# Expert 0 runs to its end before expert 1 begins, its first wait is shortened, and TensorE gets filler products in two short waits

## The chip, the core and the metric

The program runs on one core of one Trainium2 chip. A core has a matrix engine (TensorE, PE in the rows), a vector engine (VectorE, DVE), a scalar engine (ScalarE, ACT), a general engine (GpSimd, POOL) and a queue engine (SyncE, SP), each with its own instruction stream, and 16 DMA engines. The metric is the device time in microseconds (us), lower is better: 508.98 us before, the median of three runs (508.8 to 509.01).

## The reference

Three stages follow one another. All are computed in float32 by the reference.

```python
# 1. attention, (2 batches, 8 heads, 768 rows, 64 wide); rows attend to rows of the same 6-bit bucket
mask   = q_bucket[..., :, None] == k_bucket[..., None, :]
scores = np.where(mask, scale * q @ k.T, -1e9)
x      = softmax(scores) @ v                        # -> x: (1536 tokens, 512)
# 2. experts: each token goes to one of 8
e_idx  = np.argmax(x @ w_gate, axis=1)
for e in range(8):
    h = np.maximum(x[e_idx == e] @ w1[e], 0.0)      # 512 -> 1024
    out[e_idx == e] = gate_w * eom[:, e] * (h @ w2[e])   # 1024 -> 512
# 3. a dense layer on all tokens
h    = out @ w_in;  s = h * softmax(h)              # 512 -> 1024
y    = ((s - mean) / sqrt(var + 1e-6) * g_ln) @ w_out     # 1024 -> 512
```

The weights w_in and w_out arrive as 64-bit floats and are decoded on the chip from their two 32-bit halves.

## The kernel before

Every product is taken as three 16-bit products (high x high, high x low, low x high), so each operand exists as a pair hi/lo. All five engines run from an instruction order that the code writes out by hand (`manual_schedule`); each engine works through its own list in that order and stops at the head of it when an operand isn't there.

**From attention to the experts.** After the last attention unit the last three token tiles (9, 10, 11) are routed one after the other: the logits (`fin_l`), the arg-max as a one-hot mask (`route_a`), counts by products with triangular and all-ones matrices (`route_mm`), then the row of each token in a scratch table `xs` (`route_b`), into which GpSimd scatters the tokens. Expert 0's tokens are not read back from that table: TensorE collects them itself. `gather_first` adds what was read early, and `gather_mm` (written `gm`) multiplies the tiles 6 to 11 by masks `gx["oh"]` which VectorE and ScalarE build (`oh`, lines 970 to 973). On this way TensorE waits twice for a mask, ahead of `gm(6, ...)` and ahead of `route_mm(3, ...)`. The four sums lie in four PSUM banks; `gather_copy` copies them out to `xw`, sums 0 and 3 on ScalarE (line 1000), sums 1 and 2 on VectorE (line 998). Sums 0 and 3 lie in the two halves of one two-bank tile.

**The experts.** The list `seq` names the order of products: `m1` is an expert's first layer (`mm1`, lines 1255 to 1257), `m2` its second (`mm2`, lines 1284 to 1286). Each is cut into four groups `g`, and each (kind, expert, group) is a slot of the loop, 64 slots in all. A first layer's group sums over the four 128-wide parts `kk` of the 512 inputs, three products each, for two blocks of 128 outputs; its result lies in one PSUM bank of a pool of eight (`ps_x`, used in turn). `ev1` makes the hidden values: ScalarE writes hi (line 1263), and one slot later VectorE writes lo (line 1264, collected in `late`). `ev2` does the same for the second layer and writes into `yT` at a column that stands in a register; these eight registers (`starts`, line 1307) are loaded on VectorE and ScalarE from the counts in `slot_i`.

**What streams beside them.** In slot `i` the loop converts a quarter `prep[i]` of a weight matrix (ScalarE hi, line 168; VectorE lo, line 172), and issues on SP the load of the quarter that is due three slots later (`w_load`, five buffers `raw`). `WD` gives the slots at which the 13 remaining pieces of w_in and w_out are decoded: ScalarE line 126, GpSimd line 131, VectorE lines 136, 142 and 147, then hi on GpSimd and lo on VectorE; their loads go out six slots ahead. `x_load(n)` (line 1164) fetches expert n's tokens from `xs` by a transposing DMA on SP. GpSimd also scatters the gate of each token tile during the first three second layers (line 1382).

## Time and profile before

| | us |
|---|---|
| median of three runs | 508.98 |
| the profiled execution's own time | 509.42 |
| its span, first to last instruction | 507.6 |
| TensorE busy in it | 493.2 (97%) |
| VectorE, ScalarE, GpSimd busy | 385.1, 319.1, 283.2 |
| attention and routing, to TensorE's first product of an expert | 0 to 242.01 |
| experts | 242.01 to 376.40 |
| dense layer, to TensorE's last product | 376.40 to about 501 |

The times of the stages are where TensorE begins their products. A matmul row's length is a modelled latency; many are in flight at once, so the spacing of the starts is what one costs. Idle times and what ended them stand in square brackets at the end of a row.

### The profile page before, as it was taken

How to read it: one execution, taken by the hardware profiler on the slowest of the kernel's cores; microseconds unless marked ns; L12 is line 12 of the kernel's file. 1: busy time of each engine (PE TensorE's matmuls, PEld its weight loads, DVE VectorE, ACT ScalarE, POOL GpSimd, SP SyncE). 2: the span in 40 equal slices, each digit the busy share in tenths (PEclk: the TensorE clock that was granted, in tenths of full speed). 3: DMA queues.
4: the chain of work that ended last, by engine and by line, in shares of the span. 5: the costliest groups of instructions: out<-in, count | busy, mean ns of one | idle time of the engine just before them, and what ended most of it. 6: DMA issues, size and time to landing. Idle time of an engine off the chain costs nothing. (4 is left out here: it accounts for less than half of the span.)

```text
span 507.6 us, 12505 instructions
## 1 busy us (share of the span) xinstructions
PE 493.2 (97%) x4716; PEld 378.0 (74%) x4716; DVE 385.1 (76%) x914; ACT 319.1 (63%) x602; POOL 283.2 (56%) x447
## 2 busy tenths in 40 slices
PE   7899999999999999999999999999999999999994
PEld 5678787878777777787999999999974444444443
DVE  7788788878989788777698889799965986656610
ACT  6878887888778787885256574578714365444421
POOL 7989899969779898825356457320242113221131
PEclk9999999999999999999999999999999999999998
DMA  8665375988765764501599999999710236432281
GB/s 265 111 207 114 122 151 149 273 171 254 133 243 109 229 156 126 152 1 64 154 263 339 253 286 270 246 311 342 267 46 0 57 69 126 101 87 62 62 146 41
DMA packets 107182, 83.21 MB, mean 164 GB/s; under 512 B 80624, under 2 KB 89456, under 8 KB 107120
## 3 DMA queue, kind: packets, MB, share of 16 engines
q1 hardware_dynamic: 104736, 76.09, 58.5%
q0 software_dynamic: 2304, 6.31, 3.3%
q8 instruction: 37, 0.61, 0.5%
q14 instruction: 25, 0.20, 0.1%
q10 hardware_dynamic: 80, 0.00, 0.0%
HBM read 51.43 MB, written 9.97 MB: 121 GB/s over the span
## 5 line engine op out<-in xcount | busy, mean ns | idle before, releaser
L654 ACT ACTIVATE p<-s,mx 128x768 f32<-128x768 f32 x96 | 95.7, 997 | 24.3 <-DVE mx L643 12.1
L639 DVE TENSOR_REDUCE mx<-s 128x1 f32<-128x768 f32 x96 | 90.8, 946 | 22.3 <-PE s L628 19.6
L668 ACT COPY pt<-t 128x384 f32<-128x384 f32 x192 | 82.0, 480 | 17.7 <-PE t L666 16.2
L666 PE MATMUL t<-ident,p 128*128 128x128 f32 x576 | 78.8, 273 | 0.5 <-ACT pt L668 0.2
L666 PEld LDWEIGHTS t<-ident,p 128*128 128x128 f32 x576 | 68.7, 141 | 10.0 <-ACT pt L668 1.0
L690 PE MATMUL v<-pt,v 128*64 128x128 f32 x1128 | 71.9, 277 | 0.0
L131 POOL TENSOR_SCALAR dm<-dm 128x512 f32<-128x512 f32 x16 | 34.2, 2138 | 60.0 <-ACT dm L126 60.0
L690 PEld LDWEIGHTS v<-pt,v 128*64 128x64 f32 x1128 | 60.6, 137 | 7.8 <-issue 6.0
L1484 PE MATMUL o<-wo,zT 128*128 128x512 f16 (+1 forms) x312 | 63.7, 363 | 0.1
L1284 PE MATMUL a<-hh,wb 128*128 128x224 f16 (+5 forms) x256 | 63.4, 251 | 0.1
L1412 PE MATMUL h<-wi,yT 128*128 128x512 f16 x288 | 63.5, 379 | 0.0
L1285 PE MATMUL a<-hh,wb 128*128 128x224 f16 (+5 forms) x256 | 63.4, 251 | 0.0
L1286 PE MATMUL a<-hh,wb 128*128 128x224 f16 (+5 forms) x256 | 63.4, 251 | 0.0
L1256 PE MATMUL a<-xw,wa 128*128 128x224 f16 (+5 forms) x224 | 55.1, 249 | 0.0
L1255 PE MATMUL a<-xw,wa 128*128 128x224 f16 (+5 forms) x224 | 55.1, 249 | 0.0
L1257 PE MATMUL a<-xw,wa 128*128 128x224 f16 (+5 forms) x224 | 55.1, 249 | 0.0
L1484 PEld LDWEIGHTS <-zT 128*128 128x128 f16 x312 | 30.5, 98 | 32.2 <-issue 0.4
L1412 PEld LDWEIGHTS <-yT 128*128 128x128 f16 x288 | 28.2, 98 | 33.7
L628 PE MATMUL s<-k,q 128*128 128x384 f16 x192 | 47.4, 328 | 1.7 <-ACT p L654 1.5
L628 PE MATMUL s<-b,cm 128*128 128x384 f16 x192 | 47.0, 326 | 1.1 <-DVE b L590 1.1
L1490 POOL DMA_INDIRECT out_dram<-o,tok x12 | 12.6, 1046 | 53.3 <-issue 42.4
L168 ACT ACTIVATE wa<-raw 128x1024 f16<-128x1024 f32 x24 | 25.3, 1055 | 19.2 <-DMA raw<-in_moe_w_dram 19.1
(278 smaller groups left out, 1011.3 us busy)
## 6 DMA issues: line engine op xcount, KB each, us to landing
raw<-in_moe_w_dram SPq DMA_DIRECT2D x64, 512.0 KB, 5.4
raww<-in_moe_w_in_dram SPq DMA_DIRECT2D x8, 512.0 KB, 6.5
raww<-in_moe_w_out_dram SPq DMA_DIRECT2D x8, 512.0 KB, 8.2
xs<-raw SPq DMA_DIRECT2D x8, 448.0 KB, 6.8
v<-in_v_dram SPq DMA_DIRECT2D x8, 384.0 KB
q<-in_q_dram SPq DMA_DIRECT2D x6, 384.0 KB, 4.8
k<-in_k_dram SPq DMA_DIRECT2D x6, 384.0 KB
cm<-q SPq DMA_DIRECT2D x14, 96.0 KB, 2.1
```

The lines of the kernel that those rows point to most:

```text
L628: nc.tensor.matmul(t[:, c, 0:SB], d[x, h][:, s], flat(d[y, h])[:, c * SB:(c + 1) * SB], start=first, stop=not first)
L639: nc.vector.tensor_reduce(out=mx[:, 0:1], in_=t[:, :, 0:SB], op=ALU.max, axis=AX.XY)
L654: nc.scalar.activation(out=p, in_=s_t.pop(i)[:, :, 0:SB], func=AF.Exp, scale=mx[:, 1:2], bias=mx[:, 2:3], accum_out=sums[j][:, qt, h:h + 1])
L666: nc.tensor.transpose(t[:, g * 128:(g + 1) * 128], p[:, c, g * 128:(g + 1) * 128], ident)
L668: nc.scalar.copy(out=pt[i][:, 3 * c:3 * c + 3], in_=t[:, 0:SB].rearrange("p (g c) -> p g c", g=3))
L690: nc.tensor.matmul(o[64 * h:64 * h + 64], vt[:, h, c], ph[h][:, c], start=(c == 0), stop=(c == NS - 1), tile_position=(0, 64 * h))
L1255: nc.tensor.matmul(ps[:, i, 0:n], w[:, 0, kk, fs], xw[:, 0, kk], start=(kk == 0), stop=False)
L1284: nc.tensor.matmul(ps, w[:, 0, f, ds], hh[:, 0, f], start=(f == 0), stop=False)
L1285: nc.tensor.matmul(ps, w[:, 0, f, ds], hh[:, 1, f], start=False, stop=False)
L1286: nc.tensor.matmul(ps, w[:, 1, f, ds], hh[:, 0, f], start=False, stop=(f == KF - 1))
L1412: nc.tensor.matmul(ps[:, c], yT[:, a, kk, ts], w_i[:, w, kk, c * 512:(c + 1) * 512], start=(kk == 0 and a == 0 and w == 0), stop=(kk == KD ...
L1484: nc.tensor.matmul(ps, zT[:, KF * a + f], w_o[:, w, f, cs], start=(f == 0 and a == 0 and w == 0), stop=(f == KF - 1 and a == 1))
```

## The change

Five things are edited.

- `emit_pv` keeps the second bank of its last PSUM tile as `gx["spare"]`, and a new function `keep_on(n)` multiplies the 16-bit identity by itself n times into it. It is called with 10 ahead of `gm(6, ...)` and with 6 ahead of `route_mm(3, ...)`. Nothing reads these products.
- Ahead of the first `mm1` two tiles of the eight-bank pool are taken and one element of each is set to zero on VectorE, so that expert 0's first group falls on the third bank. For expert 0 the parts `kk` are summed in the order 0, 1, 3, 2.
- `seq` runs expert 0's second layer directly behind its first; expert 1's first layer follows. The weight quarters of w2 for expert 2 now come ahead of those of w1 for expert 3, and `x_load(4)` moves to the third group of expert 2's first layer.
- The column registers are loaded one by one, each at the start of its expert's second layer, and not all eight ahead of the loop.
- Nine of the 13 decoding slots in `WD` move by 2 to 5 slots.

```diff
@@ emit_pv
-                pv[j, 2] = ps_s.tile([128, 2, 512], F32, tag="s", name="s")[:, 0]
+                t = ps_s.tile([128, 2, 512], F32, tag="s", name="s")
+                pv[j, 2], gx["spare"] = t[:, 0], t[:, 1, 0:128]
@@ new
+        def keep_on(n):
+            for _ in range(n):
+                nc.tensor.matmul(gx["spare"], ident16, ident16, start=True, stop=True)
@@ the order ahead of the experts
             a_("route_s")(2)
+            a_("keep_on")(10)
             gm(6, range(4))
             a_("route_a")(3)
             oh(8, True)
+            a_("keep_on")(6)
             a_("route_mm")(3, tail=True)
@@ mm1
+        for _ in range(2):
+            spare = ps_a.tile([128, 2, CAP], F32, tag="a", name="a")
+            nc.vector.memset(spare[0:1, 0, 0:1], 0.0)
...
+            ks = (0, 1, 3, 2) if e == 0 else range(KD)
...
-                for kk in range(KD):
+                for kk in ks:
@@ the experts' loop
-        starts = [nc.values_load(slot_i[0:1, 2, e:e + 1], engines=[ET.DVE, ET.Activation], min_val=0, max_val=NT,
-                                 skip_runtime_bounds_check_because=why) for e in range(E)]
-        seq = [("m1", 0), ("m1", 1)]
-        for e in range(E - 2):
+        starts = {}
+        def start(e):
+            starts[e] = nc.values_load(slot_i[0:1, 2, e:e + 1], engines=[ET.DVE, ET.Activation], min_val=0, max_val=NT,
+                                       skip_runtime_bounds_check_because=why)
+        seq = [("m1", 0), ("m2", 0), ("m1", 1), ("m1", 2)]
+        for e in range(1, E - 2):
...
-        order = [("w1", 2), ("w1", 3), ("w2", 2)]
+        order = [("w1", 2), ("w2", 2), ("w1", 3)]
...
-        WD = [0, 2, 6, 10, 14, 18, 22, 27, 32, 54, 58, 62, 66]
+        WD = [4, 7, 10, 14, 18, 22, 26, 30, 34, 54, 58, 62, 66]
...
-            n = 3 if (kd, e, g) == ("m1", 0, 2) else e + 4 if (kd, g) == ("m2", 3) else E
+            n = {("m1", 0, 2): 3, ("m1", 2, 2): 4}.get((kd, e, g), e + 4 if e and (kd, g) == ("m2", 3) else E)
...
             else:
+                if g == 0:
+                    start(e)
                 mm2(e, g, CAPS[e])
```

Three places show what this does to the order. First TensorE where the experts begin, before the change: the last product of the count (line 896) and the first products of expert 0. `raw` holds the collected tokens, `wa` the weights; the engine named in brackets is one whose work the instruction waits for.

```order
L896 MATMUL m<-hs,ones_74 128x8 [waits PE_49]
L1255 LDWEIGHTS wa [waits PE_49]
L1255 MATMUL a<-raw,wa 128x224 [waits Activation_49]
...
L1255 MATMUL a<-raw,wa 128x224 [waits DVE_49]
...
L1255 MATMUL a<-raw,wa 128x224 [waits DVE_49]
```

And the same place in the changed kernel, where the product's line is 1268:

```order
L897 MATMUL m<-hs,ones_74 128x8 [waits DVE_49]
L1268 LDWEIGHTS wa
L1268 MATMUL a<-raw,wa 128x224 [waits Activation_49]
...
L1268 MATMUL a<-raw,wa 128x224 [waits DVE_49]
...
L1268 MATMUL a<-raw,wa 128x224 [waits Activation_49]
...
L1268 MATMUL a<-raw,wa 128x224 [waits DVE_49]
```

Before, one wait for ScalarE stands at the first product and covers both of its copies; now the first product waits for one copy and the third part has a wait for ScalarE of its own.

Second, ScalarE between the last gate (`reo`) and expert 0's hidden values (`hh`), before the change:

```order
L882 ACTIVATE reo<-rosel 128x1
L1307 TENSOR_LOAD slot_i x8
L126 ACTIVATE dm<-raww 128x512
L1263 ACTIVATE hh<-a 128x448 x2
L126 ACTIVATE dm<-raww 128x512
L1263 ACTIVATE hh<-a 128x448 x2
L168 ACTIVATE wa<-raw 128x1024
```

and in the changed kernel:

```order
L883 ACTIVATE reo<-rosel 128x1
L1276 ACTIVATE hh<-a 128x448 x4
L168 ACTIVATE wa<-raw 128x1024
L126 ACTIVATE dm<-raww 128x512
L1323 TENSOR_LOAD slot_i
L168 ACTIVATE wa<-raw 128x1024
```

The eight register loads and two decoding steps no longer stand ahead of or between expert 0's four hidden groups, and one register load stands behind them.

Third, SP's queue late in the experts, around the fetch of expert 6's tokens, before the change (line 184 loads quarters of w2 of expert 4, line 182 of w1 of expert 6, line 116 a piece of w_out):

```order
L184 DMA raw<-in_moe_w_dram 128x2x512
L116 DMA raww<-in_moe_w_out_dram 128x1024
L184 ISA
L184 DMA raw<-in_moe_w_dram 128x2x512
L1164 ISA
L1164 DMA_TRANSPOSE xw<-xs 128x8x224
L184 ISA
L184 DMA raw<-in_moe_w_dram 128x2x512
L182 ISA
L182 DMA raw<-in_moe_w_dram 128x1024
```

and in the changed kernel:

```order
L184 DMA raw<-in_moe_w_dram 128x2x512
L1172 ISA
L1172 DMA_TRANSPOSE xw<-xs 128x8x224
L184 ISA
L184 DMA raw<-in_moe_w_dram 128x2x512
L116 DMA raww<-in_moe_w_out_dram 128x1024
L182 ISA
L182 DMA raw<-in_moe_w_dram 128x1024
```

The piece of w_out went from ahead of the last two quarters of w2 to behind them.

## Rows read from the trace of the kernel before

**Rows 1.** Busy time by stretch: PE, PEld, DVE, ACT, POOL, clock, DMA share, GB/s

```profile
251.00:376.00 125.00, 124.85 (x1439) 124.67 (x1438) 107.62 (x141) 74.98 (x107) 55.54 (x47) 1.00 0.95 272
376.00:500.00 124.00, 123.87 (x599) 58.15 (x597) 73.31 (x189) 51.10 (x74) 26.81 (x39) 1.00 0.37 75
500.00:507.60 7.60, 1.23 (x12) 0.86 (x9) 0.00 (x0) 0.47 (x1) 1.00 (x1) 0.72 0.09 35
```

**Rows 2.** Timeline of TensorE, first product of the experts and of expert 1

```profile
242.01 0.26 PE L1255 MATMUL a<-raw,wa 128*128 128x224 f16 x1 [1.20 <-ACT raw L1000]
...
251.21 0.26 PE L1255 MATMUL a<-xw,wa 128*128 128x224 f16 x1
```

**Rows 3.** The copies of the collected tokens: line 1000's durations (ns), then timelines

```profile
L1000 ACT CAST raw<-s x2: 532/535/538, 241.0 to 241.4; 128x448 f16<-128x448 f32 x2
...
240.99 0.97 ACT L1000 CAST raw<-s 128x448 f16<-128x448 f32 x2 [0.77 <-PE m L896]
...
241.03 1.16 DVE L998 CAST raw<-t 128x448 f16<-128x448 f32 x2 [0.91 <-PE m L896]
```

**Rows 4.** Timeline of TensorE around its two waits for masks

```profile
234.60 0.23 PE L747 MATMUL m<-rb,xt 128*128 128x160 f16 x1
235.36 0.35 PE L989 MATMUL s<-raw,xh 128*128 128x224 f16 x2 [0.53 <-DVE raw L973]
...
235.94 0.35 PE L989 MATMUL s<-raw,xh 128*128 128x224 f16 x2
236.54 0.18 PE L822 MATMUL v<-oh_all,upper 128*128 128x16 f16 x1 [0.25 <-DVE oh_all L807]
```

**Rows 5.** Timeline of TensorE, products of 128 columns at the start and in attention

```profile
2.00 2.74 PE L481 MATMUL tb<-ident 128*128 128x128 f16 x24 [2.00 <-DVE io L261]
...
232.17 1.53 PE L690 MATMUL s<-pt,v 128*64 128x128 f32 x24
```

**Rows 6.** Timelines of ScalarE and VectorE between the gates and expert 0's hidden values

```profile
248.17 0.43 ACT L882 ACTIVATE reo<-rosel 128x3 f32<-128x3 f32 x3
...
251.85 0.95 ACT L1263 ACTIVATE hh<-a 128x448 f16<-128x448 f32 x2
...
248.97 0.28 DVE L891 RECIPROCAL me<-rz 128x3 f32<-128x3 f32 x3
252.66 0.62 DVE L1264 SCALAR_TENSOR_TENSOR hh<-a,hh 128x448 f16<-128x448 f32 x1 [3.41 <-ACT hh L1263]
```

**Rows 7.** The register loads of line 1307: durations (ns, min/median/max), first and last start

```profile
L1307 ACTq TENSOR_LOAD <-slot_i x8: 274/276/477, 248.4 to 250.9; - x8
L1307 DVEq TENSOR_LOAD <-slot_i x8: 298/306/547, 249.1 to 252.0; - x8
```

**Rows 8.** Timelines around expert 4's second layer: TensorE, VectorE, ScalarE, SP

```profile
330.81 0.25 PE L1284 MATMUL a<-hh,wb 128*128 128x200 f16 x1
...
332.44 0.25 PE L1285 MATMUL a<-hh,wb 128*128 128x200 f16 x1
...
329.57 1.23 DVE L172 SCALAR_TENSOR_TENSOR wb<-raw,wb 128x1024 f16<-128x1024 f32 x1 [3.44 <-ACT wb L168]
330.71 0.75 DVE L172 SCALAR_TENSOR_TENSOR wo<-db,g,wo 128x512 f16<-128x512 f32 x1
331.37 0.57 DVE L1264 SCALAR_TENSOR_TENSOR hh<-a,hh 128x400 f16<-128x400 f32 x1
...
328.48 1.06 ACT L168 ACTIVATE wb<-raw 128x1024 f16<-128x1024 f32 x1 [4.14 <-DMA raw<-in_moe_w_dram]
...
313.19 0.47 SPq L116 DMA_DIRECT2D raww<-in_moe_w_out_dram  x1
...
315.06 6.68 SPq L1164 DMA_TRANSPOSE xw<-xs  x1
```

**Rows 9.** Timeline of VectorE, two decoding steps of one piece

```profile
334.29 0.41 DVE L136 TENSOR_SCALAR db<-dm 128x512 int32<-128x512 int32 x1
334.74 0.69 DVE L142 SCALAR_TENSOR_TENSOR db<-raww,db 128x512 int32<-128x512 int32 x1
```

More of the change, by code (lines that the diff above doesn't have):

```diff
@@ L1253, in mm1 @@
                 fs = slice((2 * g + i) * 128, (2 * g + i + 1) * 128)
-                for kk in range(KD):
-                    nc.tensor.matmul(ps[:, i, 0:n], w[:, 0, kk, fs], xw[:, 0, kk], start=(kk == 0), stop=False)
+                for kk in ks:
+                    nc.tensor.matmul(ps[:, i, 0:n], w[:, 0, kk, fs], xw[:, 0, kk], start=(kk == ks[0]), stop=False)
                     nc.tensor.matmul(ps[:, i, 0:n], w[:, 0, kk, fs], xw[:, 1, kk], start=False, stop=False)
-                    nc.tensor.matmul(ps[:, i, 0:n], w[:, 1, kk, fs], xw[:, 0, kk], start=False, stop=(kk == KD - 1))
+                    nc.tensor.matmul(ps[:, i, 0:n], w[:, 1, kk, fs], xw[:, 0, kk], start=False, stop=(kk == ks[-1]))
             return ps
```

## The prediction

> **What bounds the kernel now.** I read the busy time by stretch first, then TensorE's timeline where its starts are not evenly spaced, then the other engines at those places, and last the stretch in which a weight lands late.
>
> In the busy time by stretch the reader is to see that TensorE has nothing left to gain inside the experts or the dense layer: 124.85 of 125.00 us and 123.87 of 124.00 [rows 1]. That is also true of the spacing. Expert 0's first layer is 96 products in 251.21 - 242.01 = 9.20 us, 0.0958 each [rows 2]; 224 columns in that time are 2.34 columns per ns, so the engine streams at the upper of its two clock levels (2.4 GHz). What is left are three waits just ahead of the experts: 0.53 and 0.25 us for masks [rows 4] and 1.20 us for the copies of the collected tokens [rows 2]. The tail behind the last product, in the last 7.6 us with TensorE at 1.23 busy, is not touched by the change [rows 1].
>
> The other engines matter only through slack. VectorE is busy 107.6 of the experts' 125 us and the DMA engines 0.95 [rows 1]; they feed TensorE just in time. The tightest place I find is expert 4's second layer. Its products begin at 330.81; the 20th, at 332.44, is the first that reads the lo of the last hidden group; VectorE finishes that at 331.37 + 0.57 = 331.94. Slack: 0.50 us [rows 8].
>
> **The change part by part.**
>
> *The third wait.* The order shows that before, TensorE's first expert product waits for both copies of ScalarE, since its bank belongs to the two-bank tile that they read. They start at 240.99 and take 0.97 together, to 241.96 [rows 3]; the product starts 0.05 later, at 242.01 [rows 2]. With the group on the third bank it waits for the first copy alone: 240.99 + 0.535 = 241.53, plus 0.05 is 241.58. The new order of parts has to fit the copies. Part 1 is needed three products later, at 241.87, and VectorE's first copy ends half-way in its 1.16, at 241.03 + 0.62 = 241.65 [rows 3]. Part 3 is needed at 242.15 and ScalarE ends at 241.96. Part 2 is needed at 242.44 and VectorE ends at 242.19. All three are covered, the least by 0.14 after the 0.05. Gain 0.43 us. Its bounds: nothing, if the wait stays as it is, and 0.48, if it starts with the copy itself done and no delay. The two small writes that move the bank are on VectorE behind the gates, where three tiny instructions take 0.28 [rows 6]; they cost at most that, and not on TensorE's path, see below.
>
> *The filler products.* None is in the trace. TensorE's room ahead of the first mask: the product at 234.60 has 160 columns, 160/224 of 0.0958 = 0.07, so the engine is free at 234.67 and the next starts at 235.36: 0.69 us. Ahead of the second: 235.94 + 2 x 0.0958 = 236.13 to 236.54: 0.41 us [rows 2, 4]. The nearest rows are 24 products of 128 columns: 1.53 us at the upper level, 0.064 each, and 2.74 us at the program's start, 0.114 each (1.1 columns per ns, the lower level, 1.2 GHz) [rows 5]. At the first price ten cost 0.64 and six 0.38; both fit, by 0.05 and 0.03, and since these prices hold the last product's latency too, the true ones are lower. At the second they overrun by 0.45 and 0.27. I take the first, as the engine runs at the upper level here: cost 0. They can't shorten a wait either, since what ends it is a mask of VectorE.
> The Trainium skill, "TensorE: Matmul & The Clock Gate", section "Wait — 56ns, not 53.3ns?", gives 55.6 ns between such products at the full clock and 106.7 at half. By that the ten would take 0.56 and the six 0.33, or 1.07 and 0.64: the same result. The sum doesn't use it.
>
> *Expert 0's second layer behind its first.* This is the edit that adds a dependence. TensorE now wants the hidden values at 241.58 + 9.20 = 250.78, where before it went on to expert 1 and came back at about 260. ScalarE is free of the gates at 248.17 + 0.43 = 248.60. Before, it then loaded eight registers (first at 248.4, last at 250.9) and reached the hidden groups at 251.85; VectorE loaded its eight from 249.1 to 252.0 and reached them at 252.66 [rows 6, 7]. The order puts the hidden groups first now. Groups 0 to 2 have long been summed; ScalarE makes them by 248.60 + 3 x 0.55, about 250.2. Group 3 is summed when its last product ends, 250.68 + 0.26 = 250.94; ScalarE takes it to about 251.5. VectorE ends the gates at 248.97 + 0.28 = 249.25, the two small writes bring it to 249.53, three lo groups of 0.62 to 251.4, and the fourth runs from about 251.6 to 252.2 [rows 2, 6]. TensorE needs it at its 20th product: 250.78 + 19 x 0.0958 = 252.60. It fits by 0.4 us, so I put this at 0. Bounds: 0, and what it costs if the hidden values start no earlier than before, at 252.66: four lo groups end at 255.14, 2.5 us too late.
>
> *One register at a time.* A load costs 0.27 to 0.48 us on ScalarE and 0.30 to 0.55 on VectorE [rows 7]. One now falls into each second layer, on engines that otherwise wait for weights there: 4.14 us of ScalarE and 3.44 of VectorE for a single quarter [rows 8]. At the tight place the load of expert 4 stands behind the hidden group that matters. Cost 0; the bound is 0.55 once, if it meets a place without slack.
> The Trainium skill, "DMA: Bandwidth & Descriptors", section "Latency and other measured facts", puts a register load at about 600 ns at least, which speaks against loading singly. The trace has less [rows 7]; at 0.6 each the bound would be 0.6 and the sum the same.
>
> *The moved stream.* On SP the two weight quarters of each swapped pair keep their buffers and sizes. Expert 1's first layer comes ten us later, so its tokens gain slack; the fetch of expert 4's tokens is moved past quarters of w1 for experts 3 and 4, and needed only in slot 28. GpSimd's gate scatters come four slots earlier and are read in slot 56. What counts is the tight place. There TensorE arrives 0.43 earlier, and ahead of the hidden lo VectorE now has two decoding steps of a later piece, 0.41 + 0.69 [rows 9], in place of the 0.75 of line 172 [rows 8]: 0.35 more. Slack 0.50 - 0.43 - 0.35 = -0.28. Against that, the last quarter of w2, for which ScalarE idles 4.14 us, loses a 512 KB piece of w_out ahead of it in the queue (issued at 313.19, ahead of the 6.68 us of the token fetch); at 272 GB/s that is 1.9 us of transfer [rows 1, 8]. So between a stall of 0.28 and a slack of 1.6; I take no stall, since what the last rows wait for is that transfer.
>
> *Sum.* 509.42 for the profiled execution, less 0.43: 508.99. It lies 0.44 above the median of the runs, so the median becomes 508.98 - 0.43 = **508.55 us**. About 0.2%, 1.02 us, is what a measurement of this kernel can tell from no change, so this counts as the same.
>
> **The rivals.**
>
> *B: the gain is eaten in expert 4.* The quarter lands no earlier and the 0.28 us stall comes, perhaps with a register load of 0.55 at another place. For it: the 0.50 us of slack [rows 8]. Against it: the shorter queue. Time: 508.55 + 0.28 = 508.8, or with the load 509.4. Still the same.
>
> *C: the fillers overrun.* They run at the lower level, masks and scatters follow 0.45 + 0.27 later: 509.3. Against it: 0.0958 per product just behind them [rows 2].
>
> *D: slower, expert 0's hidden values aren't there.* Something other than the register loads holds ScalarE until about 251.85, a scatter or a buffer of the attention stage for instance. Then VectorE ends at 255.14 and TensorE stands 2.5 us at its 20th product of the second layer: 511.1. It decides from a first lo group later than 252.60 - 4 x 0.62 = 250.1; forecast is 249.5. To be slower by over 1.02 it has to begin at about 251.6. For it: both engines' first hidden rows lie that late [rows 6]. Against it: the loads fill exactly that time [rows 7].
>
> *E: faster, the clock.* TensorE's clock stays up in this profile (1.00 in the experts) [rows 1]. If it fell in timed runs behind the waits, the fillers would hold it: 96 products at the lower level take 9.2 us more, so a fall over an eighth of them costs about 1.15 in the runs before, and without it the time would be 508.55 - 1.15 = 507.4. Against it: the spacing here, and timed runs within 0.21 us.
> The Trainium skill, "TensorE: Matmul & The Clock Gate", section "What's actually happening", says that idle time drops the clock and activity releases it; by that the fillers are worth something only where the waits had cost the clock, which no row here shows.
>
> **How the numbers follow.** Forecast 0.62, own range 508.2 to 508.9; B 0.12; C 0.08; D 0.11; E 0.07. Within 0.2%: forecast, B and C less their edges, 0.79. Slower: D and the far end of B and C, 0.13. Faster: E and the near edge of the forecast, 0.08. The range for 8 in 10 takes in forecast, B, C and the near part of D and E: 507.8 to 510.2.
>
> **What would show it.** Right: the first expert product at 241.5 to 241.65 behind an idle time of about 0.75 us; the rows behind the fillers still at 235.36 and 236.54; VectorE's first hidden group at about 249.5; no idle time of TensorE in expert 0's or expert 4's second layer; the dense layer's first product at about 375.97 instead of 376.40. Wrong: products of expert 0 spaced 0.19 (clock), an idle row at its second layer's 20th product (D), or a wait for a weight quarter anywhere before the dense layer.

## The result and the profile after

| | before | after |
|---|---|---|
| median, us | 508.80 (508.14 to 509.01, 7 runs) | 512.32 (510.47 to 513.86, 7 runs) |
| profiled execution, its span | 509.42, 507.6 | 512.78, 511.0 |
| ratio after / before | | 1.0058 (95% interval 1.0042 to 1.0073) |

The change made the kernel slower by 0.4 to 0.7%. The forecast, 508.55 us and no measurable change, was wrong, and 512.32 lies outside its range of 507.8 to 510.2. The times fall into two groups, three at 510.5 to 510.8 and four at 512.3 to 513.9.

Busy time by stretch, of after; columns as in [rows 1].

```profile
251.00:376.00 125.00, 122.33 (x1385) 121.30 (x1382) 104.48 (x136) 72.19 (x101) 56.30 (x46) 0.99 0.94 272
376.00:500.00 124.00, 123.72 (x611) 58.19 (x609) 74.53 (x191) 51.48 (x75) 26.55 (x37) 1.00 0.34 73
```

Against 124.85 in [rows 1] TensorE has lost 2.5 us of the experts' 125, and its clock is no longer at 1.00 throughout. First the places that the prediction spoke of: TensorE's timeline at the two masks and at the experts' entry, then ScalarE's and VectorE's copies there (answering [rows 2 to 4]).

```profile
234.56 0.72 PE L996 MATMUL s<-ident 128*128 128x128 f16 x10
235.25 0.35 PE L990 MATMUL s<-raw,xh 128*128 128x224 f16 x2
...
236.02 0.50 PE L996 MATMUL s<-ident 128*128 128x128 f16 x6
236.44 0.18 PE L823 MATMUL v<-oh_all,upper 128*128 128x16 f16 x1
...
240.53 0.17 PE L897 MATMUL m<-hs,ones 128*128 128x8 f16 x1
240.93 0.26 PE L1268 MATMUL a<-raw,wa 128*128 128x224 f16 x1 [0.23 <-ACT raw L1006]
...
240.34 0.97 ACT L1006 CAST raw<-s 128x448 f16<-128x448 f32 x2 [0.31 <-PE s L990]
...
240.53 1.16 DVE L1004 CAST raw<-t 128x448 f16<-128x448 f32 x2 [0.59 <-PE t L990]
```

The fillers stand where the waits were, and the rows behind them start at 235.25 and 236.44 with no idle time ahead: as TensorE's own time they cost nothing. The first expert product comes at 240.93 instead of 242.01, 1.08 us earlier where 0.43 was forecast; the copies start 0.65 and 0.50 us earlier than in [rows 3]. From the start of ScalarE's first copy to the product it is 0.59 us instead of 1.02: 0.43 less, so the rest of the 1.08 is the copies' earlier start. Expert 0's hidden values, VectorE:

```profile
249.05 1.69 DVE L1277 SCALAR_TENSOR_TENSOR hh<-a,hh 128x448 f16<-128x448 f32 x3
250.90 0.62 DVE L1277 SCALAR_TENSOR_TENSOR hh<-a,hh 128x448 f16<-128x448 f32 x1 [0.16 <-ACT hh L1276]
```

They start at 249.05 (252.66 in [rows 6]) and TensorE waits nowhere in expert 0's second layer. The time goes into expert 1's. TensorE's timeline there, and the stretches by the clock (columns as in [rows 1]):

```profile
279.68 0.26 PE L1297 MATMUL a<-hh,wb 128*128 128x224 f16 x1
282.54 0.35 PE L1298 MATMUL a<-hh,wb 128*128 128x224 f16 x1 [2.60 <-DVE hh L1277]
...
283.05 0.39 PE L1298 MATMUL a<-hh,wb 128*128 128x224 f16 x1
283.24 0.39 PE L1299 MATMUL a<-hh,wb 128*128 128x224 f16 x1
...
285.65 0.26 PE L1297 MATMUL a<-hh,wb 128*128 128x224 f16 x1
285.75 0.26 PE L1298 MATMUL a<-hh,wb 128*128 128x224 f16 x1
```

```profile
282.50:285.60 3.10, 3.06 (x17) 2.43 (x17) 3.10 (x4) 2.99 (x5) 1.22 (x2) 0.50 0.81 283
285.60:288.70 3.10, 3.10 (x34) 3.07 (x33) 3.10 (x5) 1.56 (x2) 2.82 (x3) 1.00 1.03 222
```

The 20th product waits for VectorE's last hidden lo group. It starts 2.86 us behind its neighbour, 2.77 more than the spacing of 0.096; a smaller gap of the same kind just ahead costs 0.24. Behind it 17 products fit where 34 fit later: the granted clock (the column behind the engines' busy times, the share of full speed that TensorE got) is 0.50, the lower level, 1.2 GHz. From 282.54 to 285.65 are 17 spacings, 3.11 us in place of 1.63, so this costs 1.48. The sum closes: -1.08 + 2.77 + 0.24 + 1.48 = 3.41, and the spans differ by 511.0 - 507.6 = 3.4.

What VectorE did ahead of that group (VectorE, then ScalarE, of after; the last row is VectorE's for the same group in the kernel before):

```profile
271.24 1.36 DVE L172 SCALAR_TENSOR_TENSOR wb<-raw,wb 128x1024 f16<-128x1024 f32 x1 [3.13 <-ACT wb L168]
...
279.07 1.21 DVE L172 SCALAR_TENSOR_TENSOR wb<-raw,wb 128x1024 f16<-128x1024 f32 x1
280.20 0.68 DVE L172 SCALAR_TENSOR_TENSOR wi<-db,wi 128x512 f16<-128x512 f32 x1
280.81 0.41 DVE L136 TENSOR_SCALAR db<-dm 128x512 int32<-128x512 int32 x1
281.25 0.69 DVE L142 SCALAR_TENSOR_TENSOR db<-raww,db 128x512 int32<-128x512 int32 x1
281.86 0.62 DVE L1277 SCALAR_TENSOR_TENSOR hh<-a,hh 128x448 f16<-128x448 f32 x1
...
265.26 1.06 ACT L168 ACTIVATE wa<-raw 128x1024 f16<-128x1024 f32 x1 [6.10 <-DMA raw<-in_moe_w_dram]
...
270.15 1.06 ACT L168 ACTIVATE wb<-raw 128x1024 f16<-128x1024 f32 x1 [2.84 <-DMA raw<-in_moe_w_dram]
...
269.44 0.62 DVE L1264 SCALAR_TENSOR_TENSOR hh<-a,hh 128x448 f16<-128x448 f32 x1
```

From 271.24 on VectorE has no pause; a weight quarter and three decoding steps, 2.99 us, stand directly ahead of the group that TensorE waits for. Ahead of that it stood idle for a weight quarter, and ScalarE, which converts the quarters first, for their landing (6.10 and 2.84 us). Before, the same group was done at 270.06, 10.6 us ahead of its use.

SP issues these quarters behind the fetch of expert 1's tokens, and that fetch waits for the last token scatter. GpSimd's issue of that scatter and SP's issue of the fetch (SPq is SP's queue), of after, what SP's queue waited for there, and the same two issues before:

```profile
243.35 1.00 POOL L849 DMA_INDIRECT xs<-xh,slot_all  x1 [0.28 <-POOL slot_all L847]
...
247.75 1.29 SPq L1172 DMA_TRANSPOSE xw<-xs  x1
...
SPq L1172 <- DMA xs<-xh,slot_all: 39.6, 1, 39.6
...
243.43 1.00 POOL L848 DMA_INDIRECT xs<-xh,slot_all  x1 [0.28 <-issue]
...
246.45 2.52 SPq L1164 DMA_TRANSPOSE xw<-xs  x1
```

4.40 us lie between the starts, against 3.02 in the trace of before. The DMA view of after for 244 to 248 shows why. Each digit stands for 0.1 us and gives the time of all packets that start in it, in tenths of what 16 engines have in 0.1 us, so one long packet can make a 9; q8 carries instructions.

```profile
DMA  2000090009799796000030000110100000000000
q8 instruction: 1, 0.02, 2.3%
```

The first 9, at 244.5, is one packet of instructions, 0.02 MB (16 KB), that keeps one engine for 1.45 us (2.3% of 16 engines over 4 us), to 246.03. Of the scatter's 64 packets of 4 KB, 60 run from 244.9 to 245.8; the last four run one behind the other from 246.02 to 247.01. That these four stood in line on the packet's engine is inferred from these times; the records don't name a packet's engine. The same view without the fillers (e6 below):

```profile
DMA  4000000007899898100005000000000000000248
q8 instruction: 1, 0.02, 1.5%
```

Here the packet comes at 246.1, the scatter is done by 245.8, and the fetch's own packets are there at 247.7.

All twenty traces of this document go the same way. In nine the instruction packet starts ahead of the scatter's first packet and is still running when the scatter begins (after, e1 to e5, e7, e8, e10): the fetch starts 3.85 to 4.40 us behind the scatter's issue. In eleven the packet starts behind the scatter's last one: 3.02 or 3.03. And in all twenty the fetch starts 0.61 to 0.74 us behind the end of the scatter's last packet.

### The profile page after: what moved, and what is told of

It is laid out like the page before. It is cut to its first block, busy times and chain, and to the rows that moved or that the text cites. A ratio compares the mean times of both kernels' runs of the same rounds, so it can differ in the third digit from the quotient of the medians.

```text
span 511.0 us, 12541 instructions
## 1 busy us (share of the span) xinstructions
PE 495.4 (97%) x4732; PEld 380.1 (74%) x4732; DVE 385.9 (76%) x916; ACT 319.2 (62%) x602; POOL 284.5 (56%) x447
## 5 line engine op out<-in xcount | busy, mean ns | idle before, releaser
L131 POOL TENSOR_SCALAR dm<-dm 128x512 f32<-128x512 f32 x16 | 38.4, 2402 | 58.2 <-ACT dm L126 58.0
L1298 PE MATMUL a<-hh,wb 128*128 128x224 f16 (+5 forms) x256 | 64.2, 253 | 2.7 <-DVE hh L1277 2.6
L1297 PE MATMUL a<-hh,wb 128*128 128x224 f16 (+5 forms) x256 | 64.1, 253 | 0.1
L1299 PE MATMUL a<-hh,wb 128*128 128x224 f16 (+5 forms) x256 | 64.2, 253 | 0.0
```

Source lines behind the costliest of these rows:

```text
L1297: nc.tensor.matmul(ps, w[:, 0, f, ds], hh[:, 0, f], start=(f == 0), stop=False)
L1298: nc.tensor.matmul(ps, w[:, 0, f, ds], hh[:, 1, f], start=False, stop=False)
L1299: nc.tensor.matmul(ps, w[:, 1, f, ds], hh[:, 0, f], start=False, stop=(f == KF - 1))
```

## The experiments

Each line of a diff is against the changed kernel unless it says otherwise; lines are shortened and left out (`...`). The ratios in brackets, with their 95% intervals, are to the kernel before on the same chip. Several chips were used: medians are compared between runs of one chip, ratios also across chips.

### e1, e2: the entry without the new order

```diff
# e2_old_order: fillers, bank, order of parts and single register loads stay
-seq = [("m1", 0), ("m2", 0), ("m1", 1), ("m1", 2)] ...
+seq = [("m1", 0), ("m1", 1)] ...        # and order, WD, x_load as before
# e1_front_only: as well
-                if g == 0: start(e)
+starts = [nc.values_load(...) for e in range(E)]
```

> Only the edits ahead of and at the entry to the experts (fillers, third bank, order of parts); order of experts, registers and decoding slots as before. Theory (the loss is expert 1's last hidden lo group, which stands behind VectorE's weight and decoding work since expert 1 and the second layer of expert 0 changed places): the entry is 1.0 to 1.1 us earlier than before, no stall of TensorE in the experts, clock 0.996 or more, time 507.7. Rival (the fillers or the moved banks cost the time): 510 or more, with a stall or a clock loss here too.

> As the changed kernel, with the order of experts, of weight quarters, of the token fetch and the decoding slots as before: the entry's edits and the registers loaded one by one. Theory: no stall, 507.7, as the entry's edits alone. Rival (single register loads of 0.3 to 0.55 us on VectorE and ScalarE delay the hidden values or the weights): a stall in a second layer and 509 to 512.

Measured: e1 509.74 (ratio 1.0017, 1.0008 to 1.0026), e2 509.63 (1.0016, 1.0007 to 1.0025). The gain at the entry is there (240.97) and is lost at expert 1's first product, TensorE's timeline of e1:

```profile
250.07 0.26 PE L1270 MATMUL a<-raw,wa 128*128 128x224 f16 x1
251.53 0.26 PE L1268 MATMUL a<-xw,wa 128*128 128x224 f16 x1 [1.20 <-DMA xw<-xs]
```

Both miss the theory's 507.7 and its trace without a wait: expert 1's tokens land too late here even for the old order, with the fetch 4.15 and 4.16 us behind the scatter's issue. That the registers are loaded singly changes nothing in this order.

### e3, e4: VectorE's order ahead of expert 1

```diff
# e3_late_first: the lo groups at the head of a slot
         for i, (kd, e, g) in enumerate(slots):
+            run_late()
...
-            run_late()
             if kd == "m1":
# e4_wd_late
-WD = [4, 7, 10, 14, 18, 22, 26, 30, 34, ...]
+WD = [4, 14, 17, 20, 23, 26, 29, 32, 35, ...]
```

> The changed kernel, with one line moved: in each slot the lo groups of the slot before are issued first, ahead of that slot's weight quarter and decoding steps. Theory (VectorE's order): expert 1's last lo group moves ahead of 1.21 + 0.68 + 1.10 us of other work, the stall at 280 falls from 2.86 to 0 to 0.6 us, the clock stays up, time 507.7 to 508.5. Rival (weights land late by DMA): TensorE still waits over 2 us near 280, time 510 or more.

> The changed kernel, with the second and third decoding pieces of the loop moved out of slots 7 to 12 (slots 4, 14, 17, 20, 23, 26, 29, 32, 35, rest as it was). Theory (VectorE's order): about 4 us of decoding leave VectorE ahead of expert 1's last lo group, which then ends near 278.5, so no stall at 280; the decoding is denser later and may cost up to 1 us near 330 to 345: 507.7 to 508.8. Rival (weights land late by DMA): the stall of over 2 us stays, 510 or more.

Measured: e3 509.20 (1.0001, 0.9986 to 1.0016), e4 509.44 (1.0009, 0.9997 to 1.0021). Neither waits in expert 1's second layer; the list of TensorE's waits behind the entry holds one row for e3, a weight quarter that the lo groups now precede:

```profile
PE a L1270 <- DVE wa L172: 0.8, 1, 0.8
```

In both the fetch is late all the same (4.05 and 3.85 us behind the scatter's issue). So the wait at 282 needs VectorE's order, as the theory had it; weights that land late are not enough for it alone. Both medians miss the expected times (507.7 to 508.5 and 507.7 to 508.8), and half of e4's runs are at 509.86 or more.

### e5: fillers in the new wait

```diff
+            if (e, g) == (1, 0): fill = ps_a.tile([128, 2, CAP], F32, tag="a", name="a")
...
+                if (e, g, f) == (1, 0, 6):
+                    for _ in range(40): nc.tensor.matmul(fill[:, 0, 0:128], ident16, ident16, ...)
```

> The changed kernel with one thing more: in the first group of expert 1's second layer, just ahead of the products that read the last hidden pair, TensorE multiplies the identity with itself 40 times into a bank that nobody reads. Theory A (the 2.8 us wait is VectorE's last lo group and has nothing to do with TensorE; what follows the wait at 0.187 us per product is TensorE's clock having fallen to its lower level): the last lo group is still there only at about 282.5, so the time does not fall below the changed kernel's lower times (510.5 to 510.8), but no product behind it is spaced 0.187 us, and the times above 512 are gone: 510.6, all runs within 510.2 to 511.3. Rival B (the slow spacing is not the clock's answer to the wait but comes at this place of the program anyway, weights or memory): the 18 slow products are still there in some executions, times from 510.5 to 513.9 as before. Rival C (the fillers themselves delay the path): 40 at 0.064 are 2.6 us, as long as the wait, so at most 0.3 us later: 511.

Measured: 512.15 (511.46 to 512.71, 5 runs). TensorE's timeline:

```profile
279.26 2.40 PE L1301 MATMUL a<-ident 128*128 128x128 f16 x40
281.50 0.26 PE L1302 MATMUL a<-hh,wb 128*128 128x224 f16 x1
282.08 0.26 PE L1303 MATMUL a<-hh,wb 128*128 128x224 f16 x1 [0.33 <-DVE hh L1277]
282.18 0.26 PE L1304 MATMUL a<-hh,wb 128*128 128x224 f16 x1
```

Fillers and rest are 2.24 + 0.48 = 2.72 us, the wait again, and the products behind it are spaced 0.096: no lower level here, nor a granted clock under 0.997 in any of the five. The time missed the expected 510.6 all the same; this trace has a wait of 1.1 us of its own at the dense layer's first product (for yT), and why it arises was not tried.

### e6: no fillers

```diff
-            a_("keep_on")(10)
...
-            a_("keep_on")(6)
```

> The changed kernel without the two groups of filler products (10 and 6) ahead of the masks; all else stays. Theory A (the fillers cost and bring nothing: the masks end both waits): L989's product starts at 235.25 and the count's at 236.44 within 0.1, expert 0's first product at 240.9 to 241.0, the wait in expert 1's second layer 2.5 to 3 us, time as the changed kernel's, 510.5 to 513.9 with a median of about 511.8. Rival B (the fillers are what let the copies of the collected tokens start 0.5 us earlier): the first expert product at about 241.45, and the wait in expert 1's second layer shorter by the same 0.5, since VectorE's last lo group comes when it comes: same time. Rival C (the fillers hold the clock): products of expert 0 or of the count spaced 0.19 in places, 0.5 to 2 us later.

Measured: 508.84 (508.46 to 509.42, 11 runs), ratio 0.9999 (0.9990 to 1.0008). All three expectations of the time were wrong: without fillers the loss is gone, and e5, on the same chip, has 512.15. The entry is the same (240.94). SP and GpSimd, then TensorE in expert 1:

```profile
243.37 1.00 POOL L849 DMA_INDIRECT xs<-xh,slot_all  x1 [0.28 <-POOL slot_all L847]
...
246.40 1.38 SPq L1170 DMA_TRANSPOSE xw<-xs  x1
...
279.47 0.26 PE L1295 MATMUL a<-hh,wb 128*128 128x224 f16 x1
280.57 0.26 PE L1296 MATMUL a<-hh,wb 128*128 128x224 f16 x1 [0.85 <-DVE hh L1275]
```

The fetch starts 1.35 us earlier than in after, VectorE's last lo group 1.96 earlier (279.90), and a wait of 1.0 us is left. This made the new theory: the fillers' instructions, not their time. 16 products are 32 instructions (a weight load and a product each), and if the packet is TensorE's, it is due that much earlier; 16 products of expert 0 take 1.53 us, and the packet moved from 246.1 to 244.5.

The Trainium skill, "Runtime: NRT & Kernel Launch", section "Instruction fetch mechanics", says that an engine's instructions are refilled in blocks of 16 KiB, 256 instructions, over a DMA queue, and that crossing a block is mostly hidden. The size agrees with the rows. That it is hidden holds here for TensorE, which has no wait beside the packet, and not for the scatter, whose end comes 1.2 us later (247.0 instead of 245.8).

### e7, e8: registers at once, and both cures of VectorE's order

```diff
# e7_regs_wd: e4_wd_late, and
-                if g == 0: start(e)
+starts = [nc.values_load(...) for e in range(E)]
# e8_both: the WD of e4_wd_late, and
         for i, (kd, e, g) in enumerate(slots):
+            run_late()
...
-            run_late()
```

> The changed kernel with the late decoding slots of e4_wd_late (no wait in expert 1 there) and, against that run, all eight column registers loaded ahead of the loop as before the change. Theory A (the order of expert 0's second layer needs the registers loaded one by one): ScalarE loads from about 248.2 to 250.7, VectorE from 248.9 to 251.8, the first hidden lo ends at about 252.4 and TensorE wants it at 250.2, so it waits 2.3 us in all in the first products of expert 0's second layer: e4_wd_late's 508.2 to 509.4 plus 2.3, so 510.5 to 511.7, up to 1.5 more where the clock falls behind the wait. Rival B (register loads are hidden, as in the old order, where e1_front_only and e2_old_order were the same): no wait there, 508.2 to 510 as e4_wd_late.

> The changed kernel with both cures at once: VectorE writes the hidden lo groups at the head of each slot (e3_late_first) and nine of the decoding slots stand later (e4_wd_late). Theory A (the wait in expert 1 and the wait for a weight quarter at 287 are both VectorE's order, and each cure removes the other's rest): no wait of TensorE from the first expert product (240.9) to the dense layer, span 506.3 to 506.6, median 508.0 to 508.8, so 0.0 to 0.8 under the kernel before. Rival B (what keeps e3_late_first and e4_wd_late at 509.2 and 509.4 in half of their executions is something that no order of VectorE touches, transfers that land later in some executions): median 509.0 to 509.5, two groups of times near 508.2 and 510, the same as before.

Measured: e7 511.61 (1.0057, 1.0042 to 1.0072) against e4's ratio of 1.0009. TensorE's waits behind the entry:

```profile
PE a L1297 <- ACT hh L1276: 1.5, 1, 1.5
PE a L1298 <- DVE hh L1277: 1.0, 1, 1.0
```

Expert 0's second layer stands idle for 2.5 us with the registers loaded at once (2.8 beyond the spacing), at its first and second products and not at the 20th. So the new order needs this edit, and rival D of the prediction had its price; only its condition was absent. e8: 510.18 (1.0035, 1.0015 to 1.0054), no better than either cure alone, where its theory A expected 508.0 to 508.8; its trace has no wait in expert 1 but one at the dense layer's first product (1.0 us, for yT).

### e9, e10: the number of instructions, without the fillers' place

```diff
# e9_fill_warm8: fillers stay, 16 dummy products fewer at the program's start
-            for _ in range(24):
+            for _ in range(8):
                 nc.tensor.matmul(w[:, 0:128], ident16, ident16, ...)
# e10_no_fill_warm40: no fillers, 16 tiny products more there
+            for _ in range(16): nc.tensor.matmul(w[0:8, 0:8], ident16[:, 0:8], ident16[:, 0:8], ...)
```

> The changed kernel with both groups of fillers, but 8 instead of 24 dummy products at the program's start (line 481), so that TensorE has executed as many instructions at the experts as in e6_no_fill. New theory A (not the fillers' time but their number matters: in the DMA view one instruction packet of 16 KB runs from 244.59 to 246.03 in the changed kernel, in the middle of the last token scatter, whose last packets then end at 247.0 and not at 245.8; SP starts the fetch of expert 1's tokens 4.40 us behind the issue of the last scatter and not 3.03 as without fillers; all that follows on SP, and the weights that VectorE converts ahead of expert 1's lo groups, comes over 1 us later): the packet now runs at about 246.2, the fetch starts 3.0 us behind the last scatter's issue, the wait in expert 1's second layer is about 1 us and the time that of e6_no_fill, 508.5 to 509.4. Rival B (fillers delay in another way, by TensorE's activity in the two waits): the fetch 4.0 to 4.4 us behind, 510.5 to 513. Rival C (fewer dummy products at the start leave the clock low for longer): attention later by 0.5 to 2 us, the first expert product at 241.5 or later.

> e6_no_fill (no fillers in the waits) with 16 tiny products (8 rows of 8 columns) more behind the 24 dummy products at the program's start, so that TensorE has executed as many instructions at the experts as in the changed kernel. Theory A (the number of instructions decides where the instruction packet falls): the packet runs at about 244.6 again, the last scatter's packets end 1 us later, the fetch of expert 1's tokens starts 4.0 to 4.4 us behind the last scatter's issue, the wait in expert 1's second layer is 2.3 to 3 us, time 510.5 to 513. Rival B (the fillers' place in the waits matters): as e6_no_fill, the fetch at 3.0 us, 508.5 to 509.4. The 16 products themselves cost at most 1 us at the start.

Measured: e9 510.35 (508.62 to 512.97, 12 runs; ratio 1.0023), e10 513.08 (511.06 to 514.29, 6 runs; 1.0070). SP and GpSimd of e9, with fillers, and then the list of TensorE's waits in e10, without:

```profile
245.50 1.00 POOL L849 DMA_INDIRECT xs<-xh,slot_all  x1 [0.28 <-POOL slot_all L847]
...
248.53 1.29 SPq L1172 DMA_TRANSPOSE xw<-xs  x1
```

```profile
PE a L1298 <- DVE hh L1277: 1.9, 1, 1.9
```

e9's fetch starts 3.03 us behind the scatter and nothing waits in expert 1; e10's starts 3.90 behind (251.18 and 247.28). Fillers without the delay, and the delay without fillers: for the delay it is the count. Neither time is clean, because both reach the experts late, at 243.07 and 244.85. In e9 products are spaced at the lower level to 9.7 us; its time missed theory A (508.5 to 509.4), and rival C, a slower start, came true beside it. In e10 the tiny products account for 0.6 us, the rest arises later in attention, which can be late without an edit to it: e18 below begins the experts at 242.93.

### e11, e12: the parts without fillers

```diff
# e11_bank_only, against before
+        for _ in range(2):
+            spare = ps_a.tile([128, 2, CAP], F32, tag="a", name="a")
+            nc.vector.memset(spare[0:1, 0, 0:1], 0.0)
...
+            ks = (0, 1, 3, 2) if e == 0 else range(KD)
...
-                for kk in range(KD):
+                for kk in ks:
# e12_no_fill_wd: the diff of e6_no_fill, and
-WD = [4, 7, 10, 14, 18, 22, 26, 30, 34, ...]
+WD = [4, 14, 17, 20, 23, 26, 29, 32, 35, ...]
```

> The kernel before with the change of bank and of the order of parts for expert 0 alone: no fillers, old order of the experts, registers loaded at once. Theory A (e1_front_only lost its gain of 1.08 us at the experts' entry because its fillers put the instruction packet into the last scatter, so that expert 1's tokens landed at 251.45): first expert product at 240.9 to 241.0, expert 1's tokens there at 250.4 at the latest, no wait or one of under 0.3 us at expert 1's first product; 508.88 - 1.08 = 507.8 (507.4 to 508.3). Rival B (expert 1's tokens land at 251.2 to 251.5 whatever TensorE does, as in e1_front_only and e2_old_order): a wait of 1.2 us at 250, 508.7 to 509.7.

> The changed kernel without the fillers and with the late decoding slots of e4_wd_late: both causes of the wait in expert 1's second layer taken away. Theory A: no wait of TensorE between the first expert product (240.9) and the dense layer, all runs near the lower group of e4_wd_late, 507.6 to 508.3, median 507.9 (e6_no_fill's 508.84 less its wait of 1.0). Rival B (a second limit, as weights that land late in some executions): two groups near 508 and 509.5 as in e4_wd_late.

Measured: e11 508.65 (0.9992, 0.9982 to 1.0002), e12 508.60 (0.9990, 0.9979 to 1.0001). Neither trace has a wait in expert 1 (e11's first product there starts 0.23 later than evenly spaced, where e1 had 1.46 - 0.10). e11 bears out theory A of its trace, but both medians are above the expected 507.8 and 507.9. These two ratios are the lowest seen, and neither is shown to beat the kernel before.

### e13 to e16: fillers with the count put back, on one chip

```diff
# e13_fill_wide9: fillers stay, the dummy products at the start are fewer and wider
-            for _ in range(24):
-                nc.tensor.matmul(w[:, 0:128], ident16, ident16, ...)
+            for _ in range(9):
+                nc.tensor.matmul(w[:, 0:320], ident16, pw.rearrange("p a b -> p (a b)"), ...)
# e14_after_again: no edit.  e15_no_fill_again: as e6.  e16_wide9_wd: e13 with the WD of e4
```

> The changed kernel with its fillers, and at the program's start 9 dummy products of 320 columns in place of 24 of 128 (2.4 us instead of 2.5 at the lower level's rate, so the start should take as long), which takes 15 products away and leaves one more than e6_no_fill had at the experts. Theory A (the fillers cost only through the place of the instruction packet): the packet at about 246.1, the fetch of expert 1's tokens 3.0 to 3.1 us behind the last scatter's issue, wait in expert 1's second layer 0 to 1.2 us, first expert product at 240.9, time as e15 on this chip within 0.3%, 508.5 to 509.4, and 1.5 to 3 us under e14. Rival B (the fillers delay in another way): as e14, 510.5 to 513.

> The changed kernel unaltered, on the chip of e13, e15 and e16. Both theories: packet at 244.6, fetch 4.0 to 4.4 us behind the last scatter's issue, wait of 2.3 to 2.9 us in expert 1's second layer; 510.5 to 511 where the clock stays up behind the wait, 512 to 514 where it falls.

> e6_no_fill unaltered, on the chip of e13, e14 and e16. Both theories: 508.5 to 509.4, wait of 0 to 1.2 us in expert 1's second layer. If it comes out at 510.5 or above, the chip made the difference between the changed kernel and e6, and the theory of the instruction packet falls.

> e13 with the late decoding slots of e4_wd_late as well: fillers, new order, no packet in the last scatter, VectorE free ahead of expert 1's last lo group. Theory A: no wait of TensorE behind the experts' entry, 507.6 to 508.6, as e12_no_fill_wd (508.6, 507.04 to 509.95) or up to 0.5 under it, and 0.3 to 1.2 us under the kernel before on this chip. Rival B: two groups of times as in e4_wd_late, 508.2 and 510.

Measured, before on this chip 509.30: e14 510.93 (1.0029, 1.0014 to 1.0044), e15 509.29 (1.0010, 0.9996 to 1.0024), e13 510.00 (1.0012, 0.9996 to 1.0028), e16 510.06 (1.0016, 1.0002 to 1.0030). The changed kernel is the slowest again, with half of the first result's loss, and the one without fillers the fastest. e13's trace is as theory A had it (fetch 3.02 us behind, no wait in expert 1, 508.57), but half of its runs are above 510: its interval overlaps those of e14 and of e15, so that the time comes back with the count is not shown. e16 gained nothing over e13 and missed its 507.6 to 508.6; its trace has no wait behind the entry.

e14's trace is of an execution in which the loss did not come (509.82), where both theories expected the late fetch. Its DMA view for 244 to 248:

```profile
DMA  9898100000007898997207000000000000000000
q8 instruction: 1, 0.02, 2.0%
```

In it the copies at the entry started 0.96 us (ScalarE, 241.30) and 1.51 us (VectorE, 242.04) later than in the trace of after, the packet came 1.5 us later, at 246.12, and the scatter had ended at 246.08: fetch 3.02 us behind, no wait in expert 1. So the same program does or doesn't collide from one execution to another; its runs spread from 509.25 to 512.91.

| | products more than before, ahead of the experts | fetch behind the last scatter's issue, us | wait in expert 1's second layer beyond the spacing, us |
|---|---|---|---|
| before | 0 | 3.02 | none |
| e6 (no fillers, new order) | 0 | 3.03 | 1.00 |
| e15, the same | 0 | 3.03 | 0.19 |
| e9 (fillers, 16 fewer at the start) | 0 | 3.03 | none |
| e13 (fillers, 15 fewer) | 1 | 3.02 | none |
| after | 16 | 4.40 | 2.77 |
| e5 (after, with 40 in the wait) | 16 | 3.93 | 0.48 behind 2.24 of fillers |
| e10 (no fillers, 16 more at the start) | 16 | 3.90 | 2.06 |
| e1, e2 (old order) | 16 | 4.15, 4.16 | none, 1.36 at expert 1's first product |
| e3, e4, e7, e8 (VectorE's order cured) | 16 | 4.05, 3.85, 4.02, 3.97 | none |
| e11, e12, e18 (no fillers) | 0 | 3.02, 3.02, 3.03 | none |
| e16 (fillers, 15 fewer) | 1 | 3.03 | none |
| e14 (after, late entry) | 16 | 3.02 | none |

### e17, e18: how much of the entry is the edit's

```diff
# e17_before: the kernel before, no edit.  e18_bank_only_again: as e11
```

> The kernel before, unaltered, on the chip of e18. Theory A (the bank edit lets the copies start earlier): the first copy of line 1000 starts 0.35 to 0.40 us behind the start of line 896's last product, as in the trace of before, and the first expert product 1.37 behind it, while in e18 the copy starts 0.19 ahead. Rival B (when the copies start belongs to the chip or the execution): the same offset in e17 and in e18, either 0.19 ahead (first expert product 0.8 behind line 896 here, 0.40 in e18) or 0.38 behind (1.37 here, 0.95 in e18): entry gain 0.43, as forecast. Median 508.5 to 509.3 either way.

> e11_bank_only unaltered, on the chip of e17. Theory A: the first expert product 0.95 to 1.1 us earlier than in e17, measured from the start of the count's last product; median 0.6 to 1.0 under e17. Rival B: 0.40 to 0.45 us earlier; median 0.2 to 0.6 under e17, as in e11 (ratio 0.9992).

Measured: e17 509.65 and e18 509.65 (ratio of e18 to before 0.9999, 0.9989 to 1.0009). TensorE and ScalarE of e17:

```profile
240.63 0.17 PE L896 MATMUL m<-hs,ones 128*128 128x8 f16 x1
242.71 0.26 PE L1255 MATMUL a<-raw,wa 128*128 128x224 f16 x1 [1.91 <-ACT raw L1000]
...
241.69 0.97 ACT L1000 CAST raw<-s 128x448 f16<-128x448 f32 x2 [1.48 <-PE m L896]
```

The copies start 1.06 us behind the count's last product here, 0.35 behind in the trace of before, and 0.18 ahead in e18; e14 has 0.38 behind where after, the same program, has 0.19 ahead. So the start varies between traces by more than the edit's forecast gain, also within one program. Whether the edit moves it is not told apart: both traces of before are among the late ones, and of the 18 with the edit four are late, e13 to e16, all on one chip. What the edit does behind that start is plain: from the first copy's start to the first expert product it is 1.02 us in both traces of before (here 241.69 to 242.71) and 0.58 or 0.59 in all 18 with the edit. That is the forecast 0.43, as rival B had it. In time the edit gives nothing that these runs can measure (0.9992 and 0.9999).

## Why the prediction was wrong

**The third wait: right, and small beside the spread.** TensorE no longer waits for ScalarE's second copy, and it starts 0.43 us earlier behind the first copy's start in every trace (1.02 less 0.58 or 0.59). The rest of the 1.08 in the trace of after was not forecast: the copies started earlier as well, and whether by the edit or by luck is open, as their start varies between traces. By their intervals the times of e11 and e18 leave 0 to 0.9 us for the edit.

**The filler products: this step failed.** "Cost 0" was right for TensorE's time, and rival C's overrun did not come. The step counted the fillers' duration and not their 32 instructions. These brought a 16 KB instruction packet forward into the last token scatter, which put off the fetch of expert 1's tokens, and all that SP issues behind it, by 0.8 to 1.4 us. e6, e9, e10 and e14 show it from four sides: with and without fillers, the delay goes with the packet. How much of the time the packet costs is less sure: without the fillers the loss is gone (e6 0.9999, e15 1.0010), while with fillers and the count put back e13 has 1.0012 with a spread to 511.94.

**Expert 0's second layer: right.** Hidden lo groups from 249.05, forecast 249.5; no wait. Rival D's delay comes with registers loaded at once, and e7 puts that at 2.5 us, the forecast's own upper bound.

**One register at a time: right.** The loads take 0.28 to 0.56 us each again, and e1 and e2, which differ in them alone, have the same time.

**The moved stream: this step failed too.** "Expert 1's first layer comes ten us later, so its tokens gain slack" looked at its tokens and not at its hidden values. Their lo groups moved four slots later, in among decoding steps and weight quarters, while their reader stayed; the slack went from 10.6 us to under zero. "I take no stall" stands against 2.77 + 0.24 us of wait and 1.48 of lower clock in the trace. "What counts is the tight place" was taken from the order before. That place, expert 4's second layer, got easier: its last lo group ends at 329.04 and is read at 335.83 (0.50 us apart in [rows 8]). The new tight place costs 0.2 to 1 us by itself (e15, e6) and 2.1 to 2.8 us when the stream comes later (e10, after). Neither failed step loses as much alone: the late stream in the old order makes the kernel 0.16 or 0.17% slower (e2, e1), the new order without it does not, as far as can be measured (e6).

**The clock: rival E named the wrong place.** At the waits ahead of the experts, 230 to 242, the granted clock is 1.00 before and after. The lower level came behind the wait that the change made, 1.48 us in this trace. It did not come in e10 (wait of 1.9) or with the wait filled (e5). That the upper group of after's times, from 512.3, is this fall, is argued from the granted clock of those runs (0.993 or 0.994 in all four, 0.996 to 0.999 in the others) and from one trace.

**Left open:** why e13's and e4's runs spread to 510 and above when neither trace, each of a run near the low end, shows a wait in the experts; what delays the copies' start in some traces; and the wait for yT at the dense layer in e5 and e8.

## What to carry to other kernels

An instruction that costs its engine no time still moves that engine's instruction stream: when a few dummy products change a time, look for the instruction packet in the DMA view and for a transfer on the critical path that it now meets. When a block of work is moved later, list every result that it makes, with who reads it and when, not only its inputs; the tight place of the old order says little of the new one. A gain of 0.4 us at one stage is worth only what the next operand's landing leaves of it.

## What was not expected of the hardware

- One 16 KB instruction packet held a DMA engine for 0.92 to 1.52 us (the traces from 235 to 250 us), and where it started ahead of the scatter, four of the scatter's 64 packets ran only behind it: the scatter ended at 247.0 instead of 245.8.
- TensorE's granted clock went to 0.50 for 3.1 us behind an idle time of 2.6 us in which VectorE and ScalarE were busy throughout; behind one of 1.9 us in another trace it stayed at 1.00.
- The same two copies, in the same program, started 0.19 us ahead of the count's last product in one execution and 0.38 behind it in another.
